# Pairs of two chunks of one batch with whole loads, and their state sums one row earlier, in a chunked recurrence with an MLP behind it

## The chip, the cores and the metric

The kernel runs on one core of a Trainium2 chip. The metric is the device time of one execution in microseconds (us). Three runs of the kernel before took 197.34, 198.71 and 199.65 us. The profiled execution took 198.47 us; its span, from the first to the last instruction of the profile, is 196.8 us.

Engines are called as in the profile: PE (matrix products), PEld (its weight loads), DVE, ACT and POOL (elementwise work), SP (issues nearly all DMAs). PE works through its instructions in program order, and so does each other engine and SP's queue.

## What is computed

```python
# r, k, v, w: (batch 4, heads 8, sequence 768, head size 48); u: (8, 48)
for t in range(S):
    cur = einsum('bhd,bhe->bhde', u[None] * kt, vt)
    y[:, :, t] = einsum('bhd,bhde->bhe', rt, state + cur)
    state = wt[:, :, :, None] * state + einsum('bhd,bhe->bhde', kt, vt)
x = y as (batch * sequence, 384)
h = x @ w_in                      # 384 x 2048
out = max(0.01 * h, h) @ w_out    # 2048 x 384
```

The inputs are float32, the products run in bf16.

## The kernel before

A chunk is 128 positions of one batch, all heads; there are 6 chunks in each of 4 batches, 24 in all. The list seq says which chunk has which number. Chunks are worked in pairs, and a pair is called by the number n of its first chunk: n = 0 and 2 (the function pair) are the first two chunks of batches 0 and 1; n = 4, 6, ... 22 (the function late, ten pairs) each hold the same chunk c of two neighbouring batches, one batch in partitions 0 to 63 and the other in 64 to 127. Two positions next to each other stand side by side in a partition, so a descriptor moves 2 x 48 floats, 384 bytes.

A late pair goes through these steps. Eight loads (line 780), two for each of w, k, r and v, of 64 partitions each. The logarithm of w (ACT, line 793), its cumulated sums (PE, line 806, and the sums over the chunk, line 811), exponentials of them (ACT, lines 821 to 844), and their products with r and k, called rk (DVE, line 457). rk is transposed to rkT: for n = 4 and 6 by PE (line 468), for n of at least 8 by one DMA (RK_DMA, line 865). Then the scores (PE, line 906), the mask (DVE, line 981) and the row of products (PE, line 923): the masked scores times v (intra) and r times the scaled state before the chunk (inter). inter comes in two parts, one in the step of the scores and one in the row. The sums that carry the state on (PE, line 917, results in pp) stand at the end of the same row; DVE adds them to the scaled old state (line 1001), and POOL scales the new one for the next pair of these batches (sb, line 961). POOL also makes the bonus term with u (ru, lines 876 and 880; vs, line 890) and casts v (vb, line 509). DVE adds the bonus to the row's result (y, line 1014), and y goes to xT transposed, by PE for n up to 6 and by DMA above (Y_DMA, line 1022).

The MLP takes chunks in blocks of one or two (blocks, line 265). For each it runs the products with w_in (PE, line 1050), the leaky ReLU (ACT, line 1070), the products with w_out (PE, line 1081), a copy from PSUM (DVE or ACT, lines 1092 and 1094) and a store (SP, line 1100).

The order of instructions on each engine is not written by hand. Every step is entered in a Plan with the engines that can do it, an assumed cost, a priority and what it depends on; Plan.order (line 76) then plays the steps through and writes them out in the order in which it started them. The priority of a step of pair n starts from 10 n, that of an MLP step from 1000. The tables RANK and FORCE can shift a step's priority and fix its engine; before, both are empty. Pools of buffers are sized by the calls of make (lines 304 to 322); a load of pair n also waits for the cumulated sums of an earlier pair (AHEAD, line 785). In the gaps that the plan sees on PE in the first 24 us, matrix products on zeros are put (line 1126); they compute nothing that is used.

Of the kernel before, what the change touches and what calls it, by code (L numbers as in the profile page):

```python
# [218 lines left out]
RANK = {}  # L219
FORCE = {}  # L220
# [3 lines left out]
def kernel(  # L224
# [40 lines left out]
    blocks = [1, 1, 1, 1, 1, 1, 2, 2, 2, 2, 2, 2, 2, 2, 1, 1]  # L265
    assert sum(blocks) == NCH
    assert B == 4 and C > 2
    seq = [(b, c) for b in (0, 1) for c in (0, 1)]
    for c in range(C):
        for b in (2, 0):  # L270
            if c + 2 - b < C:
                seq += [(b, c + 2 - b), (b + 1, c + 2 - b)]
# [40 lines left out]
    make("m", 5, [128, 2, NP, 128], BF16)  # L313
    make("a", 1, [128, NP, 2], F32)
    make("a2", 2, [128, 2, NP], F32)
    make("s", 2, [128, NP, D], F32)
    make("sw", 1, [128, NP, 2, D], BF16)
    make("sb", 12, [128, NP, D], BF16)
    make2("y", 6, [128, H, D], BF16)
    make("g", 3, [128, NJ, max(blocks) * L], BF16)  # L320
    make("o", 2, [128, DM], F32)
    make("ps", 8, [128, 512], F32, psum)

    with tc.manual_schedule():
# [181 lines left out]
        def cast_v(P0, slots, vv, vl):  # L506
            vb = Buf("vb")
            return vb, step(
                {"POOL": 0.56}, lambda e: nc.gpsimd.tensor_copy(out=vb.t[:], in_=vv()),  # L509
                P0 + 2, deps=vl, reads=slots, takes=[vb])  # L510
# [259 lines left out]
        def late(n):  # L770
            b, c = seq[n]
            P0 = n * 10
            first, last = c == 0, c + 1 == C
# [3 lines left out]
            for i, (name, src) in enumerate((("w", w), ("k", k), ("r", r), ("v", v))):  # L777
                for x in range(2):
                    def load(e, src=src, name=name, x=x):
                        nc.sync.dma_start(  # L780
                            out=Flat(slots[name]).t.rearrange("p (h f) -> p h f", h=H)[64 * x : 64 * x + 64],
                            in_=src[b + x, :, t0 : t0 + L, :].rearrange("h (p j) d -> p h (j d)", j=2))
# [15 lines left out]
            for j in range(2):  # L798
                vb, s_vb = cast_v(P0, [slots["v"]], view("v", j), lds["v"])
                vbs.append(vb)  # L800
                s_vbs.append(s_vb)
# [70 lines left out]
            for j in range(2):  # L872
# [13 lines left out]
                for x in range(2):  # L886
                    q = slice(64 * x, 64 * x + 64)
                    s_vs[x].append(step(
                        {"POOL": 0.85},
                        lambda e, x=x, j=j, q=q, dg=dg: nc.gpsimd.tensor_tensor(  # L890
                            out=vs2[x].t[64 * j : 64 * j + 64], in0=view("v", j)()[q],
                            in1=dg.t[q].unsqueeze(2).to_broadcast([64, H, D]), op=ALU.mult),
                        P0 + 2, deps=[lds["v"][x], s_dg], reads=[slots["v"], dg], takes=[vs2[x]]))
# [3 lines left out]
            pps = [] if last else [Buf("ps", "pp"), Buf("ps", "pp")]  # L897
# [13 lines left out]
            def sums(e):  # L911
                for g in range(NP):
                    for js in range(2):
                        for x in range(len(pps)):
                            q = slice(64 * x, 64 * x + 64)
                            for par in range(2):
                                nc.tensor.matmul(  # L917
                                    pps[x].t[64 * par : 64 * par + 64, g * D : (g + 1) * D],
                                    lhsT=rk2.t[q, js, 1, 2 * g + par, :], rhs=vbs[js].t[q, 2 * g + par, :],
                                    start=(g == 0 and js == 0), stop=(js == 1), skip_group_check=True)  # L920

            def summed(x, j, cols, **k):
                nc.tensor.matmul(  # L923
                    yps[x].t[64 * j : 64 * j + 64, cols], start=(x, j) not in begun, stop=True, skip_group_check=True, **k)
                begun.add((x, j))

            def inter(flip):
                for g in range(NP):
                    for x in range(2):
                        par = x ^ flip  # L930
                        q0, h = 64 * par, 2 * g + par
                        for j in range(2):
                            summed(x, j, slice(h * D, (h + 1) * D),
                                   lhsT=rkT2.t[q0 : q0 + D, j, g, 64 * x : 64 * x + 64], rhs=sbs[x].t[q0 : q0 + D, g, :])

            def intra(e):
                for h in range(H):
                    for js in range(2):
                        for x in range(2):
                            q = slice(64 * x, 64 * x + 64)  # L940
                            for j in range(2):
                                summed(x, j, slice(h * D, (h + 1) * D), lhsT=ms[js].t[q, h % 2, h // 2, 64 * j : 64 * j + 64],
                                       rhs=vbs[js].t[q, h, :])
# [10 lines left out]
            sbs, s_sbs = [], []  # L954
            for x in range(0 if first else 2):
                s_in, s_keeps = prev[b + x]
                sb = Buf("sb")
                sbs.append(sb)
                s_sbs.append(step(
                    {"POOL": 0.45},  # L960
                    lambda e, x=x, sb=sb, s_in=s_in: nc.gpsimd.tensor_tensor(  # L961
                        out=sb.t[:], in0=s_in.t[:], in1=a2.t[:, x].unsqueeze(2).to_broadcast([128, NP, D]), op=ALU.mult),
                    P0 + 1, deps=[*s_keeps, *s_adep], reads=[s_in, a2], takes=[sb]))

            def ahead(e):
                if not first:
                    inter(0)

            def behind(e):
                if not first:  # L970
                    inter(1)

            s_sc = step(
                {"PE": 0.65 if first else 0.75}, row(behind, scores), P0 + 1, deps=[*s_T, *s_sbs], reads=[rkT2, *sbs],
                takes=[sc for js in range(2) for sc in scs[js]] + ([] if first else yps))
            ms, s_ms = [Buf("m"), Buf("m")], []
            for js in range(2):
# [14 lines left out]
            for x in range(0 if last else 2):  # L992
                sx = Buf("s")

                def state(e, x=x, sx=sx):
                    if e == "ACT":
                        nc.scalar.copy(out=sx.t[:], in_=part(pps[x].t))
                    elif first:
                        nc.vector.tensor_copy(out=sx.t[:], in_=part(pps[x].t))
                    else:  # L1000
                        nc.vector.tensor_tensor(out=sx.t[:], in0=part(pps[x].t), in1=sbs[x].t[:], op=ALU.add)  # L1001
                prev[b + x] = (sx, [step(
                    {"ACT": 0.33, "DVE": 0.35} if first else {"DVE": 0.35}, state, P0 + 2, deps=[s_yi],
                    reads=[pps[x]] + ([] if first else [sbs[x]]), takes=[sx])])
# [4 lines left out]
            for x in range(2):  # L1009
# [8 lines left out]
                rows[n + x] = out[(b + x) * S + t0 : (b + x) * S + t0 + L, :]  # L1018
# [9 lines left out]
        for n in range(0, NCH, 2):  # L1028
            if n == B:
                for which, lo, hi, pri in WEIGHTS:  # L1030
                    weight_steps(which, lo, hi, pri)
            (pair if n < B else late)(n)
# [128 lines left out]
```

## Time and profile before

| | before |
|---|---|
| three runs, us | 197.34, 198.71, 199.65 |
| profiled execution, us | 198.47 |
| span of the profile, us | 196.8 |
| PE busy | 174.4 us (89%), 3102 matrix products |
| of it products on zeros (line 1126) | 6.9 us, 33 of them on record |
| DVE busy | 110.6 us (56%) |
| ACT busy | 105.2 us (53%) |
| POOL busy | 112.5 us (57%) |
| q1, the DMA queue of the loads | 81,712 packets, 35.66 MB, 90.5% of 16 engines |
| PE idle by releaser, largest | 5.4 us for the logarithm of w (line 793), 2.0 us for y (line 1014) |

How to read it: a busy share is a mean over the whole span, in which stages with different limits follow each other, so the table does not say what bounds the kernel. The chain of waits, the windows and the timeline of SP's queue do. In the windows, the columns are the length, the busy time of each engine with its number of instructions, the granted share of the PE clock, the share of the 16 DMA engines that packets took (above 1 where packets overlap) and the GB/s moved. In a timeline, the columns are start, duration, engine, line, operation, output and input, and the number of instructions merged into the row; SPq is SP's queue of DMA issues, and the duration is that of the issue, not of the transfer.

### The profile page before, as it was taken

Reading aid. Unit: us, or ns where it says so; the run is one execution under the profiler, and the core shown is the slowest. Engines: PE = TensorE matmul, PEld = TensorE weight load, DVE = VectorE, ACT = ScalarE, POOL = GpSimd, SP = SyncE. Lnnn points to the kernel's source line nnn. Section 1 sums busy time; section 2 is a strip of 40 time slices with the busy share of each in tenths; the row PEclk is TensorE's granted clock in tenths of the full one; section 3 lists DMA queues with packets and bytes.
Section 4 is the critical chain, followed back from the end, with each engine's and each line's share of the span. In section 5 each row is a group of like instructions: output and inputs, shape, how many; then the busy total and the mean of one; then the engine's idle time right before and its main releaser. Section 6 shows DMA issues by size and latency. Waiting matters only on the chain.

```text
span 196.8 us, 7320 instructions
## 1 busy us (share of the span) xinstructions
PE 174.4 (89%) x3102; PEld 129.5 (66%) x3106; DVE 110.6 (56%) x235; ACT 105.2 (53%) x206; POOL 112.5 (57%) x162
## 2 busy tenths in 40 slices
PE   6878999699599885979879978869999999999993
PEld 2446887467397664757657766647776777777782
DVE  7668942388777768537745763749439570111211
ACT  3649695487496656348347365236464325444230
POOL 5999802198589979919939559377890540000000
PEclk9999999999999999999999999999999999999999
DMA  6999999999999989989998999989998242111112
GB/s 150 261 266 356 382 371 244 200 212 250 218 228 224 195 191 149 221 202 187 171 196 179 218 191 200 178 219 203 214 186 200 73 54 66 42 43 40 43 42 80
DMA packets 81747, 36.13 MB, mean 184 GB/s; under 512 B 74161, under 2 KB 80946, under 8 KB 81714
## 3 DMA queue, kind: packets, MB, share of 16 engines
q1 hardware_dynamic: 81712, 35.66, 90.5%
q8 instruction: 24, 0.39, 0.9%
q14 instruction: 9, 0.07, 0.2%
q10 hardware_dynamic: 2, 0.00, 0.0%
HBM read 25.17 MB, written 4.72 MB: 152 GB/s over the span
## 4 chain that ended last, share of the span: by engine, by line
PE 38%; DMA 29%; POOL 13%; SPq 5%; DVE 5%; issue 4%; ACT 2%; DVEq 0%; POOLq 0%; ACTq 0%
PE ps L1081 16%; PE ps L1050 15%; DMA in<-in_w_dram 8%; DMA in<-in_moe_w_out_dram 6%; SPq L780 5%; DMA in<-in_r_dram 5%; DMA rkT<-rk 4%; DMA in<-in_k_dram 3%; PE ps L923 3%; DMA xT<-y 3%; POOL vs L890 3%; DVE rk L457 2%; POOL ru L489 2%; POOL vb L509 1%; ACT lw L793 1%
## 5 line engine op out<-in xcount | busy, mean ns | idle before, releaser
L1070 ACT ACTIVATE g<-ps 128x512 bf16<-128x512 f32 x96 | 56.9, 598 | 52.6 <-PE ps L1050 49.7
L1050 PE MATMUL ps<-xT,w_in_b 128*128 128x128 bf16 (+1 forms) x768 | 76.7, 246 | 3.4 <-DVE y L1014 2.0
L1081 PE MATMUL ps<-w_out_b,g 128*128 128x384 bf16 (+2 forms) x400 | 76.2, 320 | 0.3 <-DVE w_out_b L412 0.3
L1050 PEld LDWEIGHTS <-w_in_b 128*128 128x128 bf16 x768 | 60.0, 98 | 15.5 <-issue 2.2
L1081 PEld LDWEIGHTS <-g 128*128 128x128 bf16 x400 | 36.3, 98 | 15.5 <-issue 0.5
L890 POOL TENSOR_TENSOR vs<-in,dg 64x384 f32<-64x384 f32 x40 | 33.0, 824 | 2.7 <-DVE y L1014 0.8
L981 DVE TENSOR_TENSOR m<-ps,maskp 128x512 bf16<-128x512 f32 x40 | 24.8, 683 | 8.9 <-PE ps L906 8.5
L876 POOL TENSOR_TENSOR ru<-in,ub 128x384 f32<-128x384 f32 x20 | 19.8, 1000 | 16.2 <-DMA in<-in_k_dram 16.1
L457 DVE TENSOR_TENSOR rk<-in,ps 128x384 bf16<-128x384 f32 x46 | 23.5, 548 | 8.1 <-DMA in<-in_r_dram 4.9
L1092 DVE COPY o<-ps 128x384 f32<-128x384 f32 (+2 forms) x17 | 9.1, 533 | 31.3 <-PE ps L1081 22.0
L509 POOL CAST vb<-in 128x384 bf16<-128x384 f32 x24 | 11.5, 505 | 16.6 <-PE ps L917 13.6
L880 POOL TENSOR_TENSOR ru<-ru,in 128x384 f32<-128x384 f32 x20 | 19.8, 998 | 0.2
L793 ACT ACTIVATE lw<-in 128x768 bf16<-128x768 f32 x10 | 8.4, 841 | 9.3 <-DMA in<-in_w_dram 9.3
L884 DVE TENSOR_REDUCE dg<-ru 128x8 f32<-128x384 f32 x20 | 10.7, 547 | 4.7 <-POOL ru L880 4.7
L1014 DVE TENSOR_TENSOR y<-ps,vs 128x384 bf16<-128x384 f32 x20 | 10.1, 549 | 0.3 <-PE ps L923 0.3
L826 DVE TENSOR_TENSOR ci<-ps,lw 128x384 f32<-128x384 f32 x10 | 5.5, 554 | 7.8 <-PE ps L811 4.2
L961 POOL TENSOR_TENSOR sb<-s,a 128x192 bf16<-128x192 f32 x18 | 8.8, 506 | 1.9 <-ACT a L820 1.4
L1001 DVE TENSOR_TENSOR s<-ps,sb 128x192 f32<-128x192 f32 x14 | 4.3, 352 | 9.6 <-PE ps L917 9.6
L923 PEld LDWEIGHTS <-rkT 48*64 48x64 bf16 x288 | 4.1, 107 | 8.2 <-issue 4.9
L923 PE MATMUL ps<-vb,m 64*64 64x48 bf16 x640 | 7.5, 187 | 1.8 <-issue 1.8
L923 PE MATMUL ps<-sb,rkT 48*64 48x48 bf16 x288 | 6.2, 192 | 3.0 <-DMA rkT<-rk 1.6
L1126 PE MATMUL ps<-zeros 128*128 128x128 bf16 (+1 forms) x33 | 6.9, 329 | 1.9 <-DVE zeros L326 1.7
(103 smaller groups left out, 173.4 us busy)
## 6 DMA issues: line engine op xcount, KB each, us to landing
out_dram<-o SPq DMA_DIRECT2D x23, 192.0 KB, 3.2
in<-in_w_dram SPq DMA_DIRECT2D x20, 192.0 KB, 5.5
in<-in_k_dram SPq DMA_DIRECT2D x20, 192.0 KB, 5.4
in<-in_r_dram SPq DMA_DIRECT2D x20, 192.0 KB, 4.9
in<-in_v_dram SPq DMA_DIRECT2D x20, 192.0 KB, 4.6
in<-in_moe_w_out_dram SPq DMA_DIRECT2D x4, 768.0 KB, 12.4
in<-in_moe_w_in_dram SPq DMA_DIRECT2D x4, 384.0 KB, 7.4
in<-in_moe_w_in_dram SPq DMA_DIRECT2D x2, 768.0 KB, 10.2
```

What stands on the lines that cost most here:

```text
L457: (nc.gpsimd if e == "POOL" else nc.vector).tensor_tensor(out=o, in0=x, in1=i, op=ALU.mult)
L509: {"POOL": 0.56}, lambda e: nc.gpsimd.tensor_copy(out=vb.t[:], in_=vv()),
L793: lambda e: nc.scalar.activation(out=lw.t[:, :, :, 0:D].rearrange("p j h d -> p h j d"), in_=Flat(slots["w"]).t.rearrange("p (h j d) -> p ...
L876: lambda e, ru=ru, j=j: nc.gpsimd.tensor_tensor(out=ru.t[:], in0=view("k", j)(), in1=ubv, op=ALU.mult),
L880: lambda e, ru=ru, j=j: nc.gpsimd.tensor_tensor(out=ru.t[:], in0=ru.t[:], in1=view("r", j)(), op=ALU.mult),
L884: lambda e, ru=ru, dg=dg: nc.vector.tensor_reduce(out=dg.t[:], in_=ru.t[:], axis=AX.X, op=ALU.add),
L890: lambda e, x=x, j=j, q=q, dg=dg: nc.gpsimd.tensor_tensor(out=vs2[x].t[64 * j : 64 * j + 64], in0=view("v", j)()[q], in1=dg.t[q].unsqueeze ...
L923: nc.tensor.matmul(yps[x].t[64 * j : 64 * j + 64, cols], start=(x, j) not in begun, stop=True, skip_group_check=True, **k)
L981: lambda e, par=par, js=js: nc.vector.tensor_tensor(out=ms[js].t[:, par, :, :], in0=scs[js][par].t[:].rearrange("p (g t) -> p g t", g=NP), ...
L1050: nc.tensor.matmul(hp.t[:, a * N : (a + 1) * N].rearrange("p (s n) -> p s n", n=L), lhsT=w_in_b[:, t, (j + a) * 128 : (j + a + 1) * 128], ...
L1070: nc.scalar.activation(out=o, in_=i, func=AF.Prelu, alpha=0.01)
L1081: nc.tensor.matmul(op.t[:, d0:d1], lhsT=g.t[:, j, off : off + 128], rhs=w_out_b[:, j, d0:d1], start=(j == 0), stop=(j == NJ - 1))
```

## The change

A late pair now holds two chunks of one batch that follow each other, instead of the same chunk of two batches. In the numbering, n = 4 is chunks 0 and 1 of batch 2, then batch 3; then chunks 2 and 3 of batches 0, 1, 2, 3; then chunks 4 and 5 of all four. The 256 positions of a pair lie together in memory, so each of w, k, r and v is one load of 128 partitions.

The second chunk of a pair needs the state behind the first, so the order of the state steps differs: the sums of pair n + 2 stand at the end of the row of products of pair n (the generator late hands its sums out with yield, and the pair ahead of it puts them in its row); DVE adds the first chunk's sums to the scaled state, POOL scales the result, and only then can the scores' step of pair n + 2, which holds a part of inter, run. Intra now multiplies by all 128 columns of the masked scores at once (32 products of 64 x 128 weights in a pair, where there were 64 of 64 x 64).

The first pair (n = 0) is worked in two halves of four heads each (PARTS). The casts of v of late pairs may go to ACT. y of pair 6 is transposed by DMA as well (Y_DMA). The blocks of the MLP, the sizes of the buffer pools and some of the plan's constants differ, and RANK and FORCE are filled: 961 shifts of priority and 70 steps with a fixed engine. Here the two tables are left out.

```diff
     RK_DMA = {8, 10, 12, 14, 16, 18, 20, 22}
-    Y_DMA = {8, 10, 12, 14, 16, 18, 20, 22}
-    PARTS = {}
+    Y_DMA = {6, 8, 10, 12, 14, 16, 18, 20, 22}
+    PARTS = {0: [(0, NP // 2), (NP // 2, NP)]}
-    LIMITS = {"hp": 2, "op": 2, "cp": 1, "ek": 3, "yy": 2, "warm": 1, "warm2": 1}
+    LIMITS = {"hp": 2, "op": 3, "cp": 1, "ek": 2, "yy": 4, "warm": 1, "warm2": 1}
-    AHEAD = 3
-    SLACK_FROM = 60
+    AHEAD = 5
+    SLACK_FROM = 50
-    LATE = 0.6
+    LATE = 0.2
-    blocks = [1, 1, 1, 1, 1, 1, 2, 2, 2, 2, 2, 2, 2, 2, 1, 1]
+    blocks = [1, 1, 1, 1, 1, 1, 2, 2, 2, 1, 2, 1, 2, 1, 2, 1, 2]
...
-    make("lw2", 1, [128, 2, H, 64], BF16)
-    make("ci", 6, [128, H, D], F32)
-    make2("rk", 7, [128, 2, H, 64], BF16)
-    make2("rkT", 4, [128, 2 * NP, 128], BF16)
-    make("vb", 2, [128, H, D], BF16)
-    make("ru", 6, [128, H, D], F32)
+    make("lw2", 4, [128, 2, H, 64], BF16)
+    make("ci", 2, [128, H, D], F32)
+    make2("rk", 4, [128, 2, H, 64], BF16)
+    make2("rkT", 6, [128, 2 * NP, 128], BF16)
+    make("vb", 6, [128, H, D], BF16)
+    make("ru", 2, [128, H, D], F32)
...
-    make("o", 2, [128, DM], F32)
+    make("o", 6, [128, DM], F32)
...
-                for x in range(2):
-                    def load(e, src=src, name=name, x=x):
-                        nc.sync.dma_start(
-                            out=Flat(slots[name]).t.rearrange("p (h f) -> p h f", h=H)[64 * x : 64 * x + 64],
-                            in_=src[b + x, :, t0 : t0 + L, :].rearrange("h (p j) d -> p h (j d)", j=2))
-                    lds.setdefault(name, []).append(step(
-                        {"SP": 0.55}, load, P0 + i * 0.1, takes=[slots[name]], wire=PART,
-                        deps=[firsts[n - AHEAD]] if n - AHEAD in firsts else []))
+                def load(e, src=src, name=name):
+                    nc.sync.dma_start(
+                        out=Flat(slots[name]).t.rearrange("p (h f) -> p h f", h=H),
+                        in_=src[b, :, t0 : t0 + 2 * L, :].rearrange("h (p j) d -> p h (j d)", j=2))
+                lds[name] = [step(
+                    {"SP": 0.65}, load, P0 + i * 0.1, takes=[slots[name]], wire=BOTH,
+                    deps=[firsts[n - AHEAD]] if n - AHEAD in firsts else [])]
...
+            info = dict(sums=sums, deps=[*s_vbs, s_rk[1, 0], s_rk[1, 1]], reads=[*vbs, rk2], takes=pps)
+            after = yield info
+            s_pp = info["step"]
...
-                            for j in range(2):
-                                summed(x, j, slice(h * D, (h + 1) * D), lhsT=ms[js].t[q, h % 2, h // 2, 64 * j : 64 * j + 64],
-                                       rhs=vbs[js].t[q, h, :])
+                            summed(x, [0, 1], slice(h * D, (h + 1) * D), lhsT=ms[js].t[q, h % 2, h // 2, :],
+                                   rhs=vbs[js].t[q, h, :])
...
+            if not first:
+                s_in, s_keeps = prev[b]
+                sbs[0], sx = Buf("sb"), Buf("s")
+                s_sbs[0] = step(
+                    {"POOL": 0.5}, lambda e: scale(e, sbs[0], lambda: s_in.t[:], 0), P0 + 1,
+                    deps=[*s_keeps, *s_adep], reads=[s_in, a2], takes=[sbs[0]])
+                s_s = step(
+                    {"DVE": 0.35}, add(sx, sbs[0], 0), P0 + 1, deps=[s_pp, s_sbs[0]], reads=[pps[0], sbs[0]], takes=[sx])
+                s_sbs[1] = step(
+                    {"POOL": 0.5}, lambda e: scale(e, sbs[1], lambda: sx.t[:], 1), P0 + 1,
+                    deps=[s_s, *s_adep], reads=[sx, a2], takes=[sbs[1]])
...
+            more = [after] if after else []
             s_yi = step(
-                {"PE": 0.6 + 0.1 * (not first) + 0.2 * (not last)}, row(ahead, intra, *([] if last else [sums])), P0 + 2,
-                deps=[*s_ms, *s_vbs, *s_T, *s_sbs, s_rk[1, 0], s_rk[1, 1]], reads=[*ms, *vbs, rk2, rkT2, *sbs],
-                takes=[*yps, *pps])
+                {"PE": 0.83 + 0.26 * len(more)}, row(intra, inter(0), *(x["sums"] for x in more)), P0 + 2,
+                deps=[*s_ms, *s_vbs, *s_T, *s_used, *(y for x in more for y in x["deps"])],
+                reads=[*ms, *vbs, rkT2, *used, *(y for x in more for y in x["reads"])],
+                takes=[*yps, *(y for x in more for y in x["takes"])])
```

More of the change, by code (lines that the diff above doesn't have):

```diff
@@ L772, in late @@
             P0 = n * 10
-            first, last = c == 0, c + 1 == C
+            first, last = c == 0, c + 2 == C
             t0 = c * L
@@ L952, in part @@
                 return t[:, 0 : NP * D].rearrange("p (g d) -> p g d", d=D)
[L954 to L971, printed above, removed]
+            def scale(e, o, i, x):
+                (nc.gpsimd if e == "POOL" else nc.vector).tensor_tensor(
+                    out=o.t[:], in0=i(), in1=a2.t[:, x].unsqueeze(2).to_broadcast([128, NP, D]), op=ALU.mult)
+            def add(o, i, x):
+                return lambda e: nc.vector.tensor_tensor(out=o.t[:], in0=part(pps[x].t), in1=i.t[:], op=ALU.add)
@@ L1026, in late @@
                 xt_steps[n] = xt_steps[n + 1] = [s_x]
[L1028 to L1032, printed above, removed]
+        for n in range(0, B, 2):
+            pair(n)
+        for which, lo, hi, pri in WEIGHTS:
+            weight_steps(which, lo, hi, pri)
+        here = late(B)
+        info = next(here)
+        info["step"] = step(
+            {"PE": 0.46}, info["sums"], B * 10 + 1, deps=info["deps"], reads=info["reads"], takes=info["takes"])
+        for n in range(B, NCH, 2):
+            there = late(n + 2) if n + 2 < NCH else None
+            info = next(there) if there else None
+            try:
+                here.send(info)
+            except StopIteration:
+                pass
+            here = there
         t_ch = 0
```

116 lines of the change are left out of this document (64 added, 52 removed), and 116 rows, old and new, of the table RANK.

## The prediction, made before the changed kernel was run

> **What bounds the kernel now.** I read the page first, for where PE is full and where the DMA is.
>
> ```profile
> span 196.8 us, 7320 instructions
> ...
> PE   6878999699599885979879978869999999999993
> ...
> PEclk9999999999999999999999999999999999999999
> DMA  6999999999999989989998999989998242111112
> GB/s 150 261 266 356 382 371 244 200 212 250 218 228 224 195 191 149 221 202 187 171 196 179 218 191 200 178 219 203 214 186 200 73 54 66 42 43 40 43 42 80
> ```
>
> The clock is full throughout. There are two stages: up to about 150 us the DMA engines are busy and PE has holes, then PE is full and the DMA nearly idle. The windows show the same, and how much the DMA moved (last two columns):
>
> ```profile
> 5.00:10.00 5.00, 4.13 (x38) 2.27 (x37) 3.47 (x7) 3.20 (x8) 4.71 (x14) 1.00 1.28 261
> 35.00:40.00 5.00, 3.30 (x38) 2.23 (x36) 1.95 (x4) 3.02 (x6) 1.32 (x2) 1.00 1.02 200
> 100.00:140.00 40.00, 34.89 (x751) 26.00 (x751) 25.07 (x51) 20.12 (x42) 27.64 (x38) 1.00 1.12 198
> 150.00:193.00 43.00, 43.00 (x606) 32.77 (x600) 12.10 (x23) 16.13 (x27) 5.18 (x8) 1.00 0.26 62
> ```
>
> At 5 to 10 us only the whole loads of 128 partitions run: 261 GB/s. At 35 to 40 us only loads of 64 partitions run, in descriptors of the same 384 bytes: 200. Third, the timeline of SP's queue: an early whole load, and a stretch of the mixed stage. From 0.8 to 149 us there is always an issue under way; the gaps are hardly 0.1 us.
>
> ```profile
> 1.31 0.57 SPq L547 DMA_DIRECT2D in<-in_k_dram  x1
> ...
> 8.87 1.44 SPq L547 DMA_DIRECT2D in<-in_v_dram  x1
> ```
>
> ```profile
> 110.60 4.28 SPq L865 DMA_TRANSPOSE rkT<-rk  x1
> 114.98 0.61 SPq L780 DMA_DIRECT2D in<-in_r_dram  x1
> 115.68 0.57 SPq L1100 DMA_DIRECT2D out_dram<-o  x1
> 116.31 1.30 SPq L780 DMA_DIRECT2D in<-in_r_dram  x1
> 117.71 0.60 SPq L780 DMA_DIRECT2D in<-in_v_dram  x1
> 118.40 1.28 SPq L1022 DMA_TRANSPOSE xT<-y  x1
> ```
>
> Last the chain of waits. It goes through that queue; its last DMA is the transposition of rk of pair 18, for which PE waits at 131 us, and from there PE alone carries the end.
>
> ```profile
> 123.18 7.93 DMA rkT<-rk
> 131.11 0.04 issue
> 131.16 0.31 PE ps L923 x16
> ```
>
> Now PE's own work. Taking the built program's products in order at the prices of the groups by form,
>
> ```profile
> L1081 PE MATMUL ps<-w_out_b,g 128*128 128x384 bf16 x368 | 73.6, 326 | 0.3 <-DVE w_out_b L412 0.3
> L1050 PE MATMUL ps<-xT,w_in_b 128*128 128x256 bf16 x384 | 51.0, 273 | 3.2 <-DVE y L1014 2.0 <-DMA xT<-y 1.2
> L1050 PE MATMUL ps<-xT,w_in_b 128*128 128x128 bf16 x384 | 25.7, 219 | 0.2 <-ACT g L1070 0.2
> L923 PE MATMUL ps<-vb,m 64*64 64x48 bf16 x640 | 7.5, 187 | 1.8 <-issue 1.8
> ```
>
> and leaving out the zeros, I get 167.9 us. The last product ended at 193.6, so PE lost 25.7 us. The same sum up to any step gives its loss by then: 12.2 at the sums of pair 4 (25.6 us of work, run at 37.8), 14.7 at the scores of pair 8, 19.7 at pair 12, 25.5 at pair 18 (105.7 us of work, run at 131.2), and no more after it. So the end is: the latest arrival of the DMA stream against PE's order, then the work that is left, then 3.2 us of copy and store (193.6 to 196.8). The execution took 198.47 us, 1.67 more than its span and 0.24 below the median of the runs.
>
> **The change on PE.** Scores, sums and inter keep their counts (320, 256, 288). Intra: 320 products of 64 x 128 weights for 640 of 64 x 64; the early pairs have that form on record (64 products, 1.5 us), 23 ns each against 7.5/640 = 12, so 320 x 23 = 640 x 12, nothing. MLP: 96 products of 128 columns at 67 ns for 48 of 256 at 133, nothing. Pair 6 loses six transpositions, 0.1 us each. Sum: 167.4. What changes is the order: the scores of pair 18 now stand behind 115.5 us of work instead of 105.7, those of pair 22 behind 138.8 instead of 130.8; up to pair 16 it is within 2 us of before.
>
> **The change on SP's queue.** 80 half loads become 40 whole ones, y of pair 6 adds a transposition, and the order moves: all 40 loads now stand ahead of rkT of pair 18, where 67 halves stood; one more transposition of y and two more stores too. So the queue to that issue:
>
> (1) To the first load of pair 6: the same bytes as before (eight early tensors, ten weight loads, pair 4): 37.5 us, as on record. The w of pair 4 passes two of the w_out loads; PE's work ahead of its sums falls from 25.6 to 21.0 us alike, so I keep 12.2 us of loss there.
> (2) Twelve whole loads and two stores. The queue is full here (a half took 0.84 on average), so the full-queue row, 1.44 + 0.05 gap: 17.9 + 1.2 = 19.1, to 56.6. Then rkT of pair 8 must be ready: its sums at 40.1 of work + 12.2, and 5 us to the products (before, 144.4 to 149.3 for pair 22): 57.3.
> (3) Mixed stage: 24 whole loads, five rkT (21.9 us for those of before), five xT at 1.55, eleven stores at 0.63, 45 gaps at 0.09. Here the price of a whole load is not on record. Below: 0.57, the second load, with room in the queue. Above: 1.44, the full queue, which is also two halves of this stage (35 took 24.8 us, so 1.42); two halves of stage (2) would be 1.67. I take the mean of the eight early ones, 9.2/8 = 1.15, which met both: 27.6 + 21.9 + 7.8 + 6.9 + 4.0 = 68.2, issue at 125.5, and 7.9 to landing as before: 133.4.
>
> PE's loss there: 133.4 - 115.5 = 17.9. Work left 167.4 - 115.5 = 51.9; end of span 133.4 + 51.9 + 3.2 = 188.5; execution 190.2 us. Ends of the price: at 1.42, 6.5 later, 196.7; at 0.57 the transposition is 14 us earlier and no longer last. Next late, by the same sum, is rkT of pair 16 (17 of the 24 loads, 106.5 + 7.9 = 114.4, behind 99.5 of work, loss 14.9) and the w of pair 14 (loss 13.9): 187.2 or 186.2. At 0.57 for these too, the 12.2 of the start would stand: 184.5.
>
> **Edits that I cost at nothing.** Halves of pair 0: about eight more DVE and ACT instructions, under the 12 us that PE loses anyway until the weights are in; uncovered, 1 to 2 us. Six casts of v (12 at 0.5 us) from POOL to ACT: both are half idle (57 and 53%). More vb buffers take away the 13.6 us in which POOL waited for the sums, but POOL does not set the end. Fewer buffers for rk, ru and ci can hold back DVE or POOL: from zero to a pair's 2 us.
>
> **The wait that is added.** The sums of the next pair end the row; then DVE adds (0.35), POOL scales (0.5), and the scores' step waits. Behind it on PE are MLP products and the next pair's sums; DVE's mask waits for the scores. PE has 4.6 to 7 us of work between the two, so 0.85 us is hidden, unless POOL is behind: below.
>
> **A rule of the skill.** The row first: 261 GB/s whole, 200 in halves. The Trainium skill, DMA: Bandwidth & Descriptors, Rules for kernel authors, says that two transfers to disjoint halves of the partitions share the same 16 engines and advises one of 128 partitions. Its fit of one DMA in the same page (Anatomy of one DMA) is a fixed part plus bytes at one rate, by which a full queue moves whole and halves equally fast; that speaks against this change, and what it would do here is the first rival. By the two windows the trace agrees with the advice rather than with the fit, but between stages that differ in more than the form of the loads.
>
> **The rivals.**
> A, slower: a whole load holds the queue as long as two halves of stage (2), 1.67 us. Then 24 x 0.52 = 12.5 us more, the transposition lands at 145.9, loss 30.4: 202.7 us. It ends above the time before from 1.50 us per load. For it: the early full queue already took 1.44. Against: 261 against 200 GB/s, and a store of 128 descriptors was issued in 0.57, a half of 512 in 0.61, so most of an issue does not grow with size. This is also the case in which whole loads do not do what they say.
> B: the state chain is late. POOL's order has two vs (0.82 each) and two ru (1.0) near each sb; behind all four the chain takes about 4.5 us more than its 0.85, some 1 to 2 us beyond PE's cover in each pair. Until pair 18 the DMA wait absorbs it, pairs 20 and 22 do not: 190.2 + 4 = 194.2.
> C: the stream stops being last, and pair 14 or 16 or the start is: 184.5 to 187.2, say 186.
>
> **How the numbers follow.** Forecast 0.55, A 0.14, B 0.20, C 0.11. The likeliest gives 190.2 us. The range reaches from C's lower end, 184.5, over the forecast's upper end (196.7) to 198.5, and leaves out A. A measurement here can tell about 1% from no change. Faster by more than that (below 196.7): the forecast but for 0.01, C, and B but for 0.05: 0.80. Slower: 0.11 of A. The same: 0.09.
>
> **What would show it.** Right: whole loads issued in 0.6 to 1.4 us; rkT of pair 18 issued near 125 us; PE waiting for it until about 133, and full after; PE idle of about 18 us in place of 25.7; over 200 GB/s from 60 to 140 us. Wrong: whole loads near 1.5 us or more; scores waiting for sb (POOL); a row waiting for sums whose casts are late; holes in PE after the last scores.

## The result, and the profile after

The kernel after took 186.69 us (median of 4 runs, 186.07 to 188.07), the kernel before 198.38 us beside it (median of 4, 197.34 to 199.65): a ratio of 0.942, 95% interval 0.934 to 0.950. The prediction was 190.2 us, with a range of 184.5 to 198.5. The profiled execution took 186.07 us, its span 184.4. Times from here on are medians of a kernel's runs, with a run left out where it lies more than 1.5% above the fastest of its kernel (one of four in five of the kernels below).

The page of after: span, PE and DMA in 40 slices of 4.6 us.

```profile
span 184.4 us, 6694 instructions
...
PE   6979889999999999999999999989999999999993
...
PEclk9999999999999999999999999999999999999999
DMA  5999999999979999999999999998790183300113
GB/s 129 293 277 295 375 369 321 311 222 297 240 198 232 235 199 276 209 190 263 227 255 125 266 242 223 330 285 139 86 150 15 46 180 108 34 13 0 46 62 110
```

The holes that PE had up to 150 us are all but gone behind the sixth slice; the DMA is full to 130 us instead of 150. The windows of after (length, busy time and number of instructions of PE, PEld, DVE, ACT, POOL, granted clock, DMA share, GB/s) say how much:

```profile
35.00:40.00 5.00, 4.75 (x53) 3.44 (x51) 4.22 (x9) 4.36 (x9) 3.74 (x4) 1.00 1.07 238
60.00:100.00 40.00, 39.50 (x675) 29.18 (x674) 29.84 (x61) 26.44 (x57) 29.77 (x39) 1.00 1.22 227
100.00:140.00 40.00, 38.97 (x667) 29.41 (x669) 22.89 (x44) 21.61 (x43) 29.59 (x37) 1.00 1.00 201
```

From 60 to 100 us PE is busy 39.50 us where it was 34.59, and the DMA moves 227 GB/s where it moved 191. The row of before:

```profile
60.00:100.00 40.00, 34.59 (x787) 25.81 (x777) 27.56 (x55) 22.04 (x44) 30.99 (x41) 1.00 1.19 191
```

Third, SP's queue up to the transposition of rk of pair 18, from the timeline (start, duration of the issue):

```profile
114.16 0.42 SPq L903 DMA_DIRECT2D in<-in_k_dram  x1
114.67 0.82 SPq L903 DMA_DIRECT2D in<-in_v_dram  x1
115.54 3.43 SPq L1242 DMA_DIRECT2D out_dram<-o  x1
119.03 0.43 SPq L903 DMA_DIRECT2D in<-in_k_dram  x1
119.55 0.96 SPq L903 DMA_DIRECT2D in<-in_w_dram  x1
120.61 1.50 SPq L1242 DMA_DIRECT2D out_dram<-o  x1
122.64 2.97 SPq L988 DMA_TRANSPOSE rkT<-rk  x1
```

A whole load is issued in 0.42 to 0.96 us here, and the store behind it takes 3.43 or 1.50: what a load does not hold in the queue, the next entry may. The two transpositions of rk issued between 120 and 135 us landed 5.0 and 5.2 us after their issue, so that of pair 18 was there by 127.8. PE came to its scores later than that, as its timeline shows (a pair's inter comes first):

```profile
129.04 0.21 PE L1051 MATMUL ps<-sb,rkT 48*64 48x48 bf16 x2
129.41 0.30 PE L1051 MATMUL ps<-sb,rkT 48*64 48x48 bf16 x14 [0.16 <-DVE rk L580]
129.54 0.64 PE L1045 MATMUL ps<-rkT 48*64 48x128 bf16 x32
```

In before PE stood still for this transposition; the 7.93 us in the chain of the prediction are the time from its issue to its landing, and PE's own wait in it was 1.57 us:

```profile
131.16 0.31 PE L923 MATMUL ps<-sb,rkT 48*64 48x48 bf16 x16 [1.57 <-DMA rkT<-rk]
```

That wait is gone. PE's loss against its own work, worked out as in the prediction: 11.6 us at the sums of pair 4 (32.57 less 21.0 us of work), 12.4 at pair 14 (its transposition landed at 101.49, PE used it at 101.53), 13.5 at the first inter of pair 18 (129.04 less 115.5), 13.9 at the last product (181.29 less 167.4). Most of what is left is the loss of the first 33 us.

### The profile page after: what moved, and what is told of

It is laid out like the page before. It is cut to its first block, busy times and chain, and to the rows that moved or that the text cites. A ratio compares the mean times of both kernels' runs of the same rounds, so it can differ in the third digit from the quotient of the medians.

```text
span 184.4 us, 6694 instructions
## 1 busy us (share of the span) xinstructions
PE 174.9 (95%) x2829; PEld 129.9 (70%) x2833; DVE 113.7 (62%) x246; ACT 109.0 (59%) x223; POOL 105.5 (57%) x147
## 4 chain that ended last, share of the span: by engine, by line
PE 54%; DMA 14%; DVE 11%; ACT 7%; POOL 6%; issue 4%; SPq 1%; DVEq 0%; ACTq 0%; POOLq 0%
PE ps L1192 22%; PE ps L1223 20%; DMA in<-in_k_dram 6%; DMA rkT<-rk 5%; DVE rk L580 4%; DMA in<-in_w_dram 3%; PE ps L1051 3%; POOL vs L1013 3%; ACT g L1212 2%; POOL ru L999 2%; PE ps L1045 2%; PE ps L591 2%; PE ps L1268 1%; ACT ps L958 1%; DVE ci L949 1%
## 5 line engine op out<-in xcount | busy, mean ns | idle before, releaser
L1192 PE MATMUL ps<-xT,w_in_b 128*128 128x128 bf16 (+1 forms) x816 | 74.0, 241 | 1.4 <-DVE rk L580 0.7
L1223 PE MATMUL ps<-w_out_b,g 128*128 128x384 bf16 (+2 forms) x400 | 72.4, 320 | 0.2
L1013 POOL TENSOR_TENSOR vs<-in,dg 64x384 f32<-64x384 f32 x40 | 33.0, 824 | 16.5 <-DVE y L1145 10.2
L1234 DVE COPY o<-ps 128x384 f32<-128x384 f32 (+1 forms) x14 | 7.6, 544 | 28.8 <-PE ps L1223 16.6
L580 DVE TENSOR_TENSOR rk<-in,ps 128x384 bf16<-128x384 f32 (+1 forms) x49 | 23.4, 521 | 2.6 <-ACT ps L734 1.1
L1007 DVE TENSOR_REDUCE dg<-ru 128x8 f32<-128x384 f32 x20 | 10.8, 547 | 5.4 <-POOL ru L1003 3.5
L1085 POOL TENSOR_TENSOR sb<-s,a 128x192 bf16<-128x192 f32 x16 | 8.0, 504 | 8.0 <-ACT a L943 7.6
L1236 ACT COPY o<-ps 128x384 f32<-128x384 f32 (+1 forms) x11 | 5.1, 460 | 10.6 <-PE ps L1223 10.6
L954 DVE TENSOR_TENSOR ci<-ps,lw 128x384 f32<-128x384 f32 x10 | 5.5, 554 | 7.3 <-PE ps L934 5.0
L1268 PE MATMUL ps<-zeros 128*128 128x512 bf16 (+1 forms) x32 | 7.5, 362 | 2.1 <-DVE zeros L449 1.7
L949 DVE TENSOR_TENSOR ci<-ps,lw 128x384 f32<-128x384 f32 x10 | 5.6, 558 | 5.1 <-ACT ps L958 3.6
L591 PE MATMUL ps<-ident,rk 128*128 128x128 bf16 x64 | 6.6, 221 | 1.4 <-DVE rk L580 1.3
L633 POOL CAST vb<-in 128x384 bf16<-128x384 f32 x12 | 5.9, 504 | 3.3 <-PE ps L1051 1.9
```

The lines of the kernel that those rows point to most:

```text
L580: (nc.gpsimd if e == "POOL" else nc.vector).tensor_tensor(out=o, in0=x, in1=i, op=ALU.mult)
L591: nc.tensor.transpose(view()[:, g, :], rk.t[:, kind, 2 * g : 2 * g + 2, :].rearrange("p h d -> p (h d)"), ident[:])
L1007: lambda e, ru=ru, dg=dg: nc.vector.tensor_reduce(out=dg.t[:], in_=ru.t[:], axis=AX.X, op=ALU.add),
L1013: lambda e, x=x, j=j, q=q, dg=dg: nc.gpsimd.tensor_tensor(out=vs2[x].t[64 * j : 64 * j + 64], in0=view("v", j)()[q], in1=dg.t[q].unsqueeze ...
L1192: nc.tensor.matmul(hp.t[:, a * N : (a + 1) * N].rearrange("p (s n) -> p s n", n=L), lhsT=w_in_b[:, t, (j + a) * 128 : (j + a + 1) * 128], ...
L1223: nc.tensor.matmul(op.t[:, d0:d1], lhsT=g.t[:, j, off : off + 128], rhs=w_out_b[:, j, d0:d1], start=(j == 0), stop=(j == NJ - 1))
```

## The experiments

My theory after the result: the form of the loads made the whole gain, and the stream then only just meets PE's order, which starts late. The rival: the new order of the steps (RANK and FORCE, with the pairs and pools made for it) made it, and the form of the loads did little. All runs, with the ratio to the kernel before on the same chip:

| run | us | ratio, 95% interval |
|---|---|---|
| after | 186.69 | 0.942, 0.934 to 0.950 |
| lower and upper halves | 201.14 | 1.020, 1.009 to 1.030 |
| halves by heads | 186.64 | 0.946, 0.940 to 0.953 |
| planner's own order | 186.62 | 0.944, 0.937 to 0.951 |
| pair 0 undivided | 184.50 | 0.934, 0.929 to 0.940 |
| before, with whole loads | 184.81 | 0.937, 0.929 to 0.946 |
| halves in pairs 12 to 22 only | 195.56 | 0.989, 0.979 to 0.999 |
| ten loads more | 198.26 | 1.004, 0.999 to 1.009 |
| sums apart, ranks kept | 213.32 | 1.082, 1.072 to 1.092 |
| own order, pair 0 undivided | 188.67 | 0.956, 0.951 to 0.961 |
| own order, sums apart | 189.57 | 0.959, 0.952 to 0.966 |
| even and odd halves | 191.24 | 0.966, 0.957 to 0.976 |
| quarters by heads | 212.96 | 1.068, 1.060 to 1.076 |

### Halves again: lower and upper partitions, and by heads

The first, in the load of a late pair:

```diff
-                    nc.sync.dma_start(
-                        out=Flat(slots[name]).t.rearrange("p (h f) -> p h f", h=H),
-                        in_=src[b, :, t0 : t0 + 2 * L, :].rearrange("h (p j) d -> p h (j d)", j=2))
+                    for x in range(2):
+                        nc.sync.dma_start(
+                            out=Flat(slots[name]).t.rearrange("p (h f) -> p h f", h=H)[64 * x : 64 * x + 64],
+                            in_=src[b, :, t0 + x * L : t0 + x * L + L, :].rearrange("h (p j) d -> p h (j d)", j=2))
```

> The kernel after, each of the 40 late whole loads issued as two loads of 64 partitions, back to back; order, buffers and work as after. Theory 1 (a whole load holds SP's queue far shorter than two halves: 0.81 us against 2 x 0.71 in the mixed stage, 1.53 against 1.67 in the stretch before it): 24 x 0.61 + 12 x 0.14 = 16 us more of queue ahead of rkT of pair 18, whose issue moves from 122.6 to about 139 and its landing to about 147; with 51.9 us of PE work left, 3.2 of tail and 1.7 around the span that is 201 to 204 us. Theory 2 (the new order of the steps made the gain, the form of the loads did little): at most 189 us.

Measured: 201.14 us, as the first theory had it. The rival (at most 189) is out: with the new pairs, order and pools all in place, halves are slower than the kernel before.

The second keeps the number of issues and their bytes, but each load has all partitions:

```diff
+                    for x in range(2):
+                        nc.sync.dma_start(
+                            out=Flat(slots[name]).t.rearrange("p (h f) -> p h f", h=H)[:, 4 * x : 4 * x + 4, :],
+                            in_=src[b, 4 * x : 4 * x + 4, t0 : t0 + 2 * L, :].rearrange("h (p j) d -> p h (j d)", j=2))
```

> The kernel after, each late whole load issued as two loads of 128 partitions by 4 heads, back to back: as many issues and bytes per issue as two halves by partitions, but all 128 partitions in each. If the number of issues sets the queue's time, this is as the run with halves of 64 partitions, within 2 us (200 us or more by theory 1). If what is slow is the 64 partitions of a transfer (200 against 261 GB/s), it stays at 187 to 190 us.

Measured: 186.64 us, the same as after. So it is not that there are two issues; it has to do with the 64 partitions of each, and the last experiments take that apart. In the mixed stage, from rkT of pair 8 to that of pair 18, SP's 48 issues by heads took 31.5 us and after's 24 whole ones 19.4, yet rkT of pair 18 was issued at 123.2 against 122.6: stores, transpositions of y and of rk took 10.1 us less in the queue (32.3 against 42.4). An issue's duration here is in part waiting for room, and that wait is only handed from entry to entry.

### Halves in the mixed stage alone

As the first run, but pairs 4 to 10 keep whole loads:

```diff
-                    for x in range(2):
+                    wide = 1 if n >= 12 else 2
+                    for x in range(0, 2, wide):
                         nc.sync.dma_start(
-                            out=Flat(slots[name]).t.rearrange("p (h f) -> p h f", h=H)[64 * x : 64 * x + 64],
+                            out=Flat(slots[name]).t.rearrange("p (h f) -> p h f", h=H)[64 * x : 64 * (x + wide)],
```

> The kernel after, with two loads of 64 partitions in place of a whole one for the 24 loads of pairs 12 to 22 only; whole for pairs 4 to 10. With halves everywhere rkT of pair 18 was issued 20.5 us later, 9.4 of it before rkT of pair 8 and 11 behind it. If halves cost the same in each stage, this lands rkT of pair 18 about 11 us later than after, of which PE's order absorbs about 1: 194 to 198 us. If the loss came from the stretch before rkT of pair 8: below 190 us.

Measured: 195.56 us. The chain of waits of this run is again that of before:

```profile
132.15 6.51 DMA rkT<-rk
```

and PE's timeline shows who waited for it, though only 0.25 us at this place:

```profile
138.70 0.45 PE L1053 MATMUL ps<-sb,rkT 48*64 48x48 bf16 x16 [0.25 <-DMA rkT<-rk]
```

The issue moved from 122.6 to 132.2, the scores of pair 18 from 129.5 to 139.0, the time by 8.9 us. The 5.6 us that the first run lost beyond this come from the halves of pairs 4 to 10, whose price I had put at 1.7 us (12 x 0.14).

### The kernel before, with whole loads and nothing else

```diff
                 for x in range(2):
                     def load(e, src=src, name=name, x=x):
-                        nc.sync.dma_start(
-                            out=Flat(slots[name]).t.rearrange("p (h f) -> p h f", h=H)[64 * x : 64 * x + 64],
-                            in_=src[b + x, :, t0 : t0 + L, :].rearrange("h (p j) d -> p h (j d)", j=2))
+                        if x == 0:
+                            nc.sync.dma_start(
+                                out=Flat(slots[name]).t.rearrange("p (h f) -> p h f", h=H),
+                                in_=src[b, :, min(t0, S - 2 * L) : min(t0, S - 2 * L) + 2 * L, :].rearrange("h (p j) d -> p h (j d)", j=2))
```

> The kernel before with its order, buffers and steps, but each pair of half loads replaced by one whole load of 128 partitions: the same bytes, from two chunks of one batch instead of one chunk of two batches, so it computes on other numbers of the same kind and its outputs are not the reference's. Theory 1 (form of the loads): the stream comes forward by 10 us or more at rkT of pair 18 and PE's loss there (25.5 us) falls towards the start's 12.2: 185 to 190 us. Theory 2 (the gain needs the new pairs, their order and the sums in the row): 196 us or more.

Measured: 184.81 us. The old pairs, the old order and the old pools give the whole gain once the loads are whole. Its windows are those of after to a few GB/s:

```profile
60.00:100.00 40.00, 38.63 (x832) 29.07 (x823) 29.46 (x61) 24.71 (x51) 34.78 (x48) 1.00 1.18 224
100.00:140.00 40.00, 38.52 (x716) 28.53 (x713) 27.00 (x54) 21.62 (x44) 26.78 (x35) 1.00 1.07 201
```

and its scores of pair 18, behind 105.7 us of work, ran at 118.17 us, a loss of 12.5 us in place of 25.5:

```profile
118.03 0.31 PE L924 MATMUL ps<-sb,rkT 48*64 48x48 bf16 x16
118.17 0.62 PE L907 MATMUL ps<-rkT 48*64 48x128 bf16 x32
```

What the new pairs are needed for is that the bytes of a whole load lie in one batch, one stretch behind the other; with the old pairs this run could do it only by reading other numbers.

### The order, and the first pair

```diff
-RANK = {0: -75.58, 1: -23.13, 2: -2.84, 3: 392.23, 4: 277.13, 5: 382.22, 6: -283.56, 7: -284.05, 8: -283.63,
...
+RANK = {}
+FORCE = {}
```

> The kernel after without the table of ranks and without the forced engines: the planner's own order and choice of engines, as the kernel before had it, and all the rest of the change. Theory 1 (whole loads): most of the gain of 11.7 us stays, 187 to 194 us, with a whole load below 1.2 us in the mixed stage. Theory 2 (the order): 197 us or more.

Measured: 186.62 us. By themselves the 961 shifts of priority and 70 fixed engines change nothing that these runs can tell; with pair 0 undivided they do, as the two runs below show together.

```diff
-    PARTS = {0: [(0, NP // 2), (NP // 2, NP)]}
+    PARTS = {}
```

With this edit the ranks stay with the steps that they belonged to; those of the second halves go.

> The kernel after with its first pair undivided: whole loads and whole steps as in the kernel before, ranks of the other steps kept. By the prediction the halves cost nothing and bring nothing that sets the end: 186 to 188 us. The rival: since PE's loss at the start (11.6 of the 13.9 us that it loses in all) now sets the end, the halves are worth what they bring forward there, and this is 1 to 3 us slower than after, with a larger loss at the sums of pair 4.

Measured: 184.50 us, faster than after by 2.2 us; neither expectation had that sign. It beats both kernels. PE's order is the same as in after, step by step, so the chains of both can be laid side by side. After: the issues of the two halves of r, the landing of the first half of k, then the state sums of pair 0 and the cumulated sums of pair 4.

```profile
1.87 0.50 SPq L671
2.41 0.51 SPq L671
2.96 4.64 DMA in<-in_k_dram
...
16.26 0.45 PE ps L782 x16
...
32.73 0.33 PE ps L929 x2
```

Pair 0 undivided, the two sums:

```profile
14.84 0.45 PE ps L793 x16
...
31.51 0.33 PE ps L945 x2
```

The sums of pair 0 come 1.4 us earlier and those of pair 4 1.2: a loss of 10.4 us instead of 11.6. In after, four half loads stand ahead of k and its first half is sent at 2.96 us; undivided, two loads stand ahead of it and all of k is sent at 1.94. The sums of pair 0 need both halves, so an early first half does not help them. That this order of the loads is the cause is read from the chains and not shown by a run of its own: undivided, the chain of the start does not pass through k at all, and in after it also holds 2.3 us of products on zeros between 10.2 and 16.3 us. The stream came forward as well: rkT of pair 18 was issued at 120.95 us instead of 122.64.

> The kernel after with the planner's own order (no ranks, no forced engines) and its first pair undivided. The own order alone measured 186.6 us and the undivided first pair alone 184.5. If the order is worth nothing and the halves cost their 2 us at the start wherever the order comes from: 184 to 185 us. If the ranks only made up for something: 186 us or more.

Measured: 188.67 us, in the second range, but not for its reason. In this order the halves make next to no difference at the start (sums of pair 4 at 35.80 us undivided, 35.95 in halves) nor by the last copy of the output (0.19 us). The span is still 186.4 against 184.9 us; the difference is behind the last product, in the last stores. Why they land later I have not found. What the halves of pair 0 cost is so shown only for the order with the ranks. Read the other way, with pair 0 undivided the ranks and fixed engines are worth 4.2 us (184.50 against 188.67): their last product ends 2.8 us earlier (179.34 against 182.16).

### More bytes

Each late pair's v is loaded a second time into one of two scratch buffers that nothing reads.

```diff
-                    nc.sync.dma_start(
-                        out=Flat(slots[name]).t.rearrange("p (h f) -> p h f", h=H),
+                    for o in [slots[name]] + ([extra[n // 2 % 2]] if name == "v" else []):
+                        nc.sync.dma_start(
+                            out=(Flat(o).t if o is slots[name] else o[:]).rearrange("p (h f) -> p h f", h=H),
```

> The kernel after, with the v of each late pair loaded a second time into a scratch buffer that nothing reads: ten whole loads more, 0.39 MB each. If the stream is close to being last (rkT of pair 14 landed within 0.1 us of PE's need), nine of them at 1.5 to 1.7 us each (bytes at the 227 to 240 GB/s of the windows from 40 to 100 us) lie ahead of rkT of pair 18: 12 to 15 us later, 196 to 200 us. If the stream has slack: at most 189 us.

Measured: 198.26 us, 11.6 more than after; rkT of pair 18 issued at 135.3, 12.7 later. So after has no room left in the stream: it is a bound beside PE's late start, and less work at the start alone would soon meet it.

### The sums in a row of their own

```diff
-            more = [after] if after else []
             s_yi = step(
-                {"PE": 0.83 + 0.26 * len(more)}, row(intra, inter(0), *(x["sums"] for x in more)), P0 + 2,
+                {"PE": 0.83}, row(intra, inter(0)), P0 + 2, deps=[*s_ms, *s_vbs, *s_T, *s_used],
...
+            if after:
+                after["step"] = step(
+                    {"PE": 0.26}, after["sums"], P0 + 2, deps=after["deps"], reads=after["reads"], takes=after["takes"])
```

> The kernel after, with the state sums of the next pair as a step of their own behind the row of products instead of the end of the row: the row no longer waits for the next pair's casts and products. If the row's wait costs (the second rival of the prediction): 1 to 4 us faster than after, 183 to 186 us. If it is hidden, as PE's waits of after suggest (none above 1.3 us in all): within 1 us of after, 186 to 187.5 us.

Measured: 213.32 us. Outside both expectations, and no test of the row's wait: with a step more, the planner played the ranks into another order (scores of pair 16 behind 113.8 us of PE's work, 99.5 in after), and rkT of pair 16 was issued at 119.0 instead of 103.6. The granted clock was lower too, 0.50 from 100 to 110 us. So the same edit without ranks:

> The kernel after with the planner's own order and the next pair's state sums as a step of their own. The run with the sums apart and the ranks kept was 27 us slower, with PE's order changed throughout (scores of pair 16 behind 113.8 us of work instead of 99.5); here the scores stay within 2 us of the own order with the sums in the row, and the sums come 1 to 6 us earlier. If it was the order that cost: within 1.5 us of the 186.6 of the own order. If sums of their own cost by themselves: 190 us or more. If the row's wait costs: below 185 us.

Measured: 189.57 us against 186.62 with the sums in the row. Between my bounds, but on the slower side: giving the sums a step of their own gains nothing, so the row's wait costs nothing that this would free. Whether the sums themselves or the order cost the 3 us stays open.

### What makes a half slow

```diff
+                    for x in range(2):
+                        nc.sync.dma_start(
+                            out=Flat(slots[name]).t.rearrange("p (h f) -> p h f", h=H)[x : 128 : 2],
+                            in_=src[b, :, t0 : t0 + 2 * L, :].rearrange("h (p x j) d -> x p h (j d)", x=2, j=2)[x])
```

> The kernel after, each late whole load as two loads of 64 partitions back to back as in the first experiment, but of the even and of the odd partitions instead of the lower and the upper 64. If what is slow is the number of partitions of a transfer: as with lower and upper halves, 199 to 204 us. If it is that the 64 lie side by side: as with halves by heads, 186 to 189 us.

Measured: 191.24 us, between the two: about 10 us of the 14.5 go when 64 partitions no longer lie side by side, 4.5 stay. Windows of the mixed stage, 60 to 120 us, in four kernels. After:

```profile
60.00:120.00 60.00, 59.37 (x1012) 44.35 (x1011) 39.37 (x79) 36.48 (x77) 42.53 (x54) 1.00 1.19 234
```

Lower and upper halves in pairs 12 to 22:

```profile
60.00:120.00 60.00, 53.44 (x954) 38.71 (x942) 36.82 (x74) 31.77 (x66) 38.03 (x49) 1.00 1.16 192
```

Halves by heads:

```profile
60.00:120.00 60.00, 58.74 (x1005) 43.83 (x1003) 39.24 (x78) 36.14 (x76) 41.43 (x53) 1.00 1.14 231
```

Even and odd halves:

```profile
60.00:120.00 60.00, 56.07 (x960) 40.94 (x958) 37.77 (x76) 32.17 (x67) 42.19 (x53) 1.00 0.98 208
```

The last two columns tell two causes apart. With lower and upper halves the DMA engines are as busy as in after (1.16 against 1.19) and move 192 GB/s instead of 234: the packets themselves take longer. With even and odd halves the engines are less busy (0.98): they wait for work, which points at SP's queue. Two rows of SP's timeline, two halves each, the first by heads:

```profile
87.32 1.08 SPq L904 DMA_DIRECT2D in<-in_w_dram  x2
```

and the second with even and odd halves:

```profile
90.47 1.29 SPq L904 DMA_DIRECT2D in<-in_w_dram  x2
```

The shortest such pairs in the two runs took 1.00 us by heads and 1.28 by even and odd partitions. Whether SP's time is the second cause, the last run asks: the loop by heads over four loads of two heads.

```diff
-                    for x in range(2):
+                    for x in range(4):
...
-                            out=Flat(slots[name]).t.rearrange("p (h f) -> p h f", h=H)[:, 4 * x : 4 * x + 4, :],
+                            out=Flat(slots[name]).t.rearrange("p (h f) -> p h f", h=H)[:, 2 * x : 2 * x + 2, :],
```

> The kernel after, each late whole load as four loads of 128 partitions by 2 heads, back to back: 160 issues where the kernel before had 80 and after has 40, the same bytes. Two loads by 4 heads cost the queue at least 2 x 0.50 us and changed nothing (186.6 us). If SP's issue time is the second thing that halves cost (even and odd halves: at least 2 x 0.64 us a pair, 191.4 us): four at 0.45 to 0.5 make 1.8 to 2.0 us a tensor, 0.5 to 0.7 more than even and odd halves, 12 to 17 us more over the 24 loads of the mixed stage: 200 to 208 us. If only bytes and their place in the partitions count: at most 189 us.

Measured: 212.96 us, above the range expected; 96 issues took 53.3 us of the mixed stage, 2.2 us a tensor. The window of this kernel, with the engines least busy of all:

```profile
60.00:120.00 60.00, 48.88 (x833) 35.36 (x833) 35.01 (x71) 30.02 (x63) 36.69 (x47) 0.94 0.92 182
```

So SP's issue time is a bound of its own: at 2 x 0.50 us a tensor it hides behind the bytes, at 4 x 0.49 it does not. That the 2 x 0.64 of even and odd halves make the 4.5 us that stay fits both windows, but is argued from them, not shown alone.

The Trainium skill, SBUF — State Buffer, section Door 1: The DMA port swizzle, says that the partitions from 0 to 63 reach only 8 of the 16 ports through which DMAs write, those from 64 to 127 the other 8, and that four neighbouring partitions share a port. By that rule even and odd halves reach all 16. The trace agrees with the direction: 192 GB/s against 234, and most of the loss gone with even and odd halves; the page's own pair of readings, 196 against 328 GB/s, is wider apart than these mixed stages are.

## Why the prediction was right, and where its sizes were off

**The bound and the direction** were right: two stages, the first bound by the stream of loads, and whole loads bring it forward. The run with whole loads in the kernel before shows it with nothing else changed but the numbers that the loads read.

**PE's work** was right: the busy time of after, without its zeros, is 174.9 - 7.5 = 167.4 us. The way that the prediction names does not lead there, though. Groups by form overlap in time, so busy time divided by count prices a product too high: the four rows shown alone add up to 157.8 of the 167.9 us. That sum agrees instead with PE's busy time of before without the zeros (174.4 - 6.9 = 167.5), and the 105.7 us of work up to the scores of pair 18 with the busy time by then (112.07 - 6.9 = 105.2), so the losses stand. Intra's form cost nothing: 32 products of 128 columns in 0.51 us by their starts (0.53 for 64 of 64 columns before). The start's loss was kept at 12.2 us; it was 11.6.

**Stage (2)** of the queue: 12 loads at 1.49 us were predicted and took 1.53; rkT of pair 8 was issued at 55.5, for 57.3. The queue of before was read as a little fuller than it is: beside the gaps of hardly 0.1 us it has three of 1.33, 0.51 and 0.73 us, at 40, 69 and 89 us.

**Stage (3)** came out right as a sum and wrong in its terms: 67.2 us for 68.2. The 24 loads took 19.4 us (0.81 each) where I put 27.6 (1.15 each); the eleven stores took 10.8 for 6.9, the five xT 9.5 for 7.8, the rkT 22.0 for 21.9. The mean of the early loads was too high a price, and the stores' price from before too low, since both hold the wait for room; that the errors cancel to 1 us is luck.

**The step that failed** is the arrival at pair 18: issue 125.5, "landing +7.9 = 133.4, loss 17.9". Issue was at 122.6 (1.8 us from the earlier start of the stage, 1.0 from its length) and the landing 5.2 us behind it instead of 7.9, so the data was there at 127.8, 5.6 us sooner, and PE, which came at 129.0, did not wait for it until 133 as the prediction's signs had it. The mis-sized terms are small, and the largest is the landing, which I took over from a stage with a fuller stream. With them rival C came true (184.5 to 187.2): the stream is no longer last, the loss is 13.9 us instead of 17.9, and that is 4.0 of the 4.1 us between 190.2 and the profiled 186.07. So the range held because it reached down to a rival that had been given a chance of 0.11.

**Rival A** (a whole load as dear as two halves) is refuted with numbers at hand: in the mixed stage 0.81 us against 1.55 for two halves (46 halves took 35.6 us in the run with halves in pairs 12 to 22). **Rival B** did not show: PE has no wait for sb in after, and the sums apart gained nothing.

**An edit costed at nothing** was not nothing: the halves of pair 0. The prediction covered them with "the 12 us that PE loses anyway until the weights are in". The loss at the start is not a wait for the weights alone: the sums of pair 0 came 1.4 us later with halves, and 1.2 of it lived on to pair 4 and 1.8 to the end of the span (184.4 against 182.6). Its uncovered price, 1 to 2 us, was the right size, but by luck: it was meant for some more instructions on DVE and ACT, and the chains point at the order of the loads.

**The rule weighed** in the prediction: the Trainium skill, DMA: Bandwidth & Descriptors, has in Rules for kernel authors the advice of one transfer of 128 partitions, and in Anatomy of one DMA a fit by bytes, which the page gives for DMAs issued from GpSimd; the loads here come from SP. Halves by heads agree with the fit (186.64 us), halves of lower and upper partitions with the advice (201.14). Which partitions a transfer covers decided here, not whether it was one of two.

## What to carry to other kernels

Price a load by two things read apart: the DMA engines' time for its bytes (share and GB/s in the windows) and SP's time to issue it; the larger one bounds, and a queue's issue durations alone do not say which, since they hold the wait for room. Where a tile is filled by halves of its partitions, first try whether the loop can be turned so that one load, or each of two, spans all partitions; here that was worth all of the 6%, and the new order changed nothing until pair 0 was undivided. When a bound is moved, ask what was hidden under it: here a split of the first pair that had seemed free.

## What the runs showed of the hardware that was not expected

The shortest issue of a late load was 0.60 us for 64 partitions by 8 heads (lower and upper, or even and odd), and 0.37 to 0.38 us for 128 partitions, by 8, 4 or 2 heads alike: in these runs it went with the partitions and hardly with the bytes. The share of the DMA engines' time per GB/s, from the four windows above and with the stores and transpositions in them, was 0.0060 for lower and upper halves (1.16/192), and 0.0047 to 0.0051 for whole loads, halves by heads, and even and odd halves (1.19/234, 1.14/231, 0.98/208): the side-by-side 64 partitions alone cost the engines more. The granted clock, 1.00 in after, was 0.91 from 100 to 120 us in the run with quarters, where PE was busy 17.16 of 20 us, and 0.50 from 100 to 110 us in the run with the sums apart and the ranks kept, where it was busy 4.40 of 10. The run with halves in pairs 12 to 22 shows more idle time than the first at 1.00 (16.73 of 20 us busy from 100 to 120), so the idle time of a stretch alone does not explain it, and no run here was made to find out.
